# Attention, dense branch and residual added in PSUM: the sum in four column groups of TensorE instead of one

## The chip, the cores and the metric

The kernel runs on one core of a Trainium2 chip. The metric is the device time of one execution in microseconds. The kernel before took 192.61 us (median of 4 runs, 192.52 to 193.02). The engines are named as in the profile: PE is the matrix engine (PEld its weight loads, which have records of their own), DVE the vector engine, ACT the scalar engine, POOL the general one, and SP the engine that issues most DMA transfers here. PSUM is the accumulator memory that matmuls write, in banks; SBUF is the working memory.

## The reference

Two rows (one token of each of two batch entries, 448 numbers) are normalised, and two branches are added to the input:

```python
xn = _layernorm(x)                         # x: (2, 1, 448), bf16
# branch A: one query token against the last W = 4096 entries of a cache of 32768
q = (xn @ wq) -> 16 heads of 256;  k, v: 8 kv heads, each for two query heads
p = softmax(q k^T * 256**-0.5);  o = p v;  A = o.reshape(2, 4096) @ wo       # wo: (4096, 448)
# branch B: a dense layer with mish
h = xn @ w1 + b1;  B = (h * tanh(softplus(h))) @ w2                          # w1: (448, 1792)
out = x + A + B
```

Nearly all of the data is the window of the two caches: for each of 16 pairs of kv head and batch entry 4096 x 256 numbers of k and as many of v, 2 MB each. All inputs are bf16.

## The kernel before

**Loads.** All large loads go through the queue that SP issues. k has four buffers, v and the weights share five, wo has three. A pair's k and v tiles hold 32 cache entries on each of the 128 partitions. The order on SP is: wq (two parts), k of pair 0, w1, w2, k of pairs 1 and 2, and then in turn k two pairs ahead, v of this pair, and after each second pair that kv head's part of wo. The last v comes in three parts (half, a quarter, a quarter), the last wo in two (one for each of the kv head's two query heads), and these are the last loads.

**A pair.** Pairs are worked in two halves of 2048 cache entries. For each half DVE transposes k in 32x32 blocks (`turn`, L356), PE makes the scores with eight matmuls of 512 columns (`scores`, L368), ACT takes the exponential and row sums (L378), and DVE transposes the result (`turn_p`, L389). Two pairs later (`KA = 2`) `values` multiplies with v: 64 matmuls of two columns, whose weights are v itself (L415), into a tile `po`. DVE divides by the softmax's sum into `oT` (L426), which holds 128 partitions x 2 halves of the head x 2 query heads x 2 batch entries in bf16. When both batch entries of a kv head are done, `mix` multiplies `oT` by that kv head's part of wo.

**The sum.** All of the output's terms are added in PSUM, in two tiles `psA[0]` and `psA[1]` of 2 rows (batch entries) and 224 columns, in a bank each. The helper `add` (L206) is one matmul: the weights are two columns (one for each batch entry), and 224 columns of the other factor stream through. It is called for x itself (2 matmuls with an identity as weights), in `dense_out` for the dense branch (28, from pair 1 on in the order of work), and in `mix` (8 for each of 8 kv heads). In `mix` the loops run over query head, then bank, then half of the head, so that of the last eight matmuls the sixth ends bank 0 and the eighth bank 1.

**The end.** DVE copies `psA[0]` into columns 0 to 223 of `res`, ACT copies `psA[1]` into columns 224 to 447, and SP stores `res`, two rows of 896 bytes (L487 to L489).

**Order.** The instructions of each engine stand in the order of the program text; `issue_in_order` fixes it. An engine that waits holds up all that stands behind it.

Of the kernel before, what the change touches and what calls it, by code (L numbers as in the profile page):

```python
# [12 lines left out]
FP32 = mybir.dt.float32  # L13
# [21 lines left out]
def kernel(  # L35
# [13 lines left out]
    nc = tc.nc  # L49
    P = 128  # L50
    Q = 32
    NQ = P // Q

    Bsz, Sq, D = A_x.shape
    _, Hkv, Sk, Dh = A_k_cache.shape
    HqDh = A_wq.shape[1]
    Hq = HqDh // Dh
    rep = Hq // Hkv
# [12 lines left out]
    ND = Dh // P  # L71
# [8 lines left out]
    ident = lead.tile([P, P], BF16)  # L80
# [11 lines left out]
    ps_a = ctx.enter_context(tc.tile_pool(name="ps_a", bufs=1, space=PSUM))  # L92
# [3 lines left out]
    x_bf = consts.tile([Bsz, D], BF16)  # L96
# [5 lines left out]
    def v_tile(n):  # L102
        t = v_pool.tile([P, T * Dh], BF16, tag="v", name="v")
        return t[:, 0:n]
# [6 lines left out]
    for lo, hi in ((0, SC), (SC, NS)):  # L111
        w = v_tile((hi - lo) * HW).rearrange("p (s n) -> p s n", n=HW)
# [15 lines left out]
        out=rstd[:], in_=mv[:, 1:2], func=ACT.Sqrt, bias=eps_t[:], scale=1.0  # L128
# [5 lines left out]
    for r in range(2):  # L134
        n = (NS + 1 - r) // 2
        nc.vector.tensor_scalar(  # L136
            out=xn_bf[:, r : NS : 2, :, :],
# [12 lines left out]
    for b4 in range(NB):  # L150
        rows = slice(b4 * Q, (b4 + 1) * Q)
        for j in range(NQ):
            nc.vector.tensor_copy(
                out=spread[rows, b4, j * Q : (j + 1) * Q], in_=ident[rows, rows]
# [3 lines left out]
    for j in range(1, NQ):  # L158
        nc.vector.tensor_tensor(
            out=hsel, in0=hsel, in1=ident[:, j * Q : j * Q + rep], op=ALU.add  # L160
# [12 lines left out]
    for s in range(NS):  # L173
# [7 lines left out]
        out=odd[:],  # L181
        in_=ident[:].rearrange("p (u o) -> p o u", o=2),
# [4 lines left out]
    for par in range(2):  # L187
        for x in range(NX):
            which = (par + x) % 2
            nc.vector.tensor_scalar(  # L190
                out=xs[:, par : NS : 2, x, :],
# [6 lines left out]
    nc.vector.memset(ones[:], 1.0)  # L198


    NO = 2
    DO = D // NO
    psA = [ps_a.tile([Bsz, DO], FP32, name=f"psA{n}") for n in range(NO)]

    def add(n, lhsT, rhs, **flags):
        nc.tensor.matmul(psA[n][:, :], lhsT=lhsT, rhs=rhs, skip_group_check=True, **flags)  # L206

    for n in range(NO):
        add(n, ident[0:Bsz, 0:Bsz], x_bf[:, n * DO : (n + 1) * DO], start=True, stop=False)


    qrep = consts.tile([P, NB, HH, NE, NX, Bsz], BF16)
# [42 lines left out]
    act_bf = consts.tile([P, NF, NX, Bsz], BF16)  # L255
# [53 lines left out]
    def dense_out():  # L309
        w2_sb = dense.pop("w2")  # L310
        for x in range(NX):
            for c in range(NF):
                for n in range(NO):
                    add(
                        n,
                        act_bf[:, c, x, :],
                        w2_sb[:, x, c, n * DO : (n + 1) * DO],
                        start=False,
                        stop=False,
                    )  # L320


    NSTEP = len(heads) * NH
# [109 lines left out]
    def mix(kvh):  # L433
        oT = state["oT"]
        w = wo_t.pop(kvh)
        for h in range(rep):
            for n in range(NO):
                for c in range(ND):
                    add(
                        n,  # L440
                        oT[:, c, h, :],
                        w[:, h, c * D + n * DO : c * D + (n + 1) * DO],
                        start=False,
                        stop=(kvh == Hkv - 1 and h == rep - 1 and c == ND - 1),
                    )

    NK = len(heads)
    KA = 2
# [8 lines left out]
    for i in range(NK + KA):  # L457
        if i + 2 < NK:
            load_k(i + 2)
        if i < NK:  # L460
            load_v(i, (0, T) if i < NK - 1 else (0, T // 2, 3 * T // 4, T))
            kvh, b = heads[i]
            if b == Bsz - 1:
                load_wo(kvh, parts=1 if i < NK - 1 else 2)
            for half in range(NH):
                s = i * NH + half
                if s + 1 < NSTEP:
                    turn(s + 1)
                scores(s)
                if s >= 1:  # L470
                    turn_p(s - 1)
            if i + 2 < NK:
                build_q(i + 2)
        if i == NK:
            turn_p(NSTEP - 1)
        if i == 0:
            dense_in()
        if i == 1:
            dense_out()
        if i >= KA:  # L480
            values(i - KA)
            kvh, b = heads[i - KA]
            if b == Bsz - 1:
                mix(kvh)

    res = consts.tile([Bsz, D], BF16)
    nc.vector.tensor_copy(out=res[:, 0:DO], in_=psA[0][:, :])  # L487
    nc.scalar.copy(out=res[:, DO:D], in_=psA[1][:, :])  # L488
    nc.sync.dma_start(out=out.flatten_outer_dims(), in_=res[:])  # L489
    issue_in_order(tc)  # L490

# [29 lines left out]
```

The softmax here doesn't subtract the row's maximum and nothing guards it: scores larger than these inputs give would overflow.

## Time and profile before

| what | us |
| --- | --- |
| median of 4 runs | 192.61 (192.52 to 193.02) |
| the profiled execution, whole | 192.56 |
| its span from first to last instruction | 190.7 |
| PE busy, matmuls (1592) | 129.1 |
| DVE busy | 108.5 |
| ACT busy | 25.4 |
| last part of v has landed | 185.54 |
| last eight matmuls of the sum, start and length | 186.43, 1.67 |
| store issued | 188.49 |

The profile is one execution. A line of a timeline gives start and duration in microseconds, the engine, the line of the code, the operation, what it writes and reads with the shapes, and in brackets the idle time of the engine before it and what ended that. "128*2" at a matmul is rows x columns of the weights. "PEclk" and the clock column of windows are the clock that PE was granted: 1.00 is full, 0.50 half. Times that follow from single records are given to two or three decimals.

### The profile page before, as it was taken

Reading aid. Unit: us, or ns where it says so; the run is one execution under the profiler, and the core shown is the slowest. Engines: PE = TensorE matmul, PEld = TensorE weight load, DVE = VectorE, ACT = ScalarE, POOL = GpSimd, SP = SyncE. Lnnn points to the kernel's source line nnn. Section 1 sums busy time; section 2 is a strip of 40 time slices with the busy share of each in tenths; the row PEclk is TensorE's granted clock in tenths of the full one; section 3 lists DMA queues with packets and bytes.
Section 4 is the critical chain, followed back from the end, with each engine's and each line's share of the span. In section 5 each row is a group of like instructions: output and inputs, shape, how many; then the busy total and the mean of one; then the engine's idle time right before and its main releaser. Section 6 shows DMA issues by size and latency. Waiting matters only on the chain.

```text
span 190.7 us, 3752 instructions
## 1 busy us (share of the span) xinstructions
PE 129.1 (68%) x1592; PEld 75.7 (40%) x1592; DVE 108.5 (57%) x169; ACT 25.4 (13%) x69; POOL 25.1 (13%) x139
## 2 busy tenths in 40 slices
PE   0251991599876939397639766794949493895974
PEld 0151390145553616244334524361625333362672
DVE  4706406895949390939366663939092764849301
ACT  5000110111210211011100211021102011021100
POOL 8005220020220202002020202020200200000000
PEclk9999995769997996579856995599658879589965
DMA  6999999999999999999999999999999999999970
GB/s 231 424 436 418 432 435 426 426 428 421 431 438 423 430 416 440 426 426 417 449 426 419 423 433 431 430 440 419 426 423 430 421 442 423 437 425 431 402 280 7
DMA packets 7818, 77.90 MB, mean 409 GB/s; under 512 B 757, under 2 KB 2809, under 8 KB 3322
## 3 DMA queue, kind: packets, MB, share of 16 engines
q1 hardware_dynamic: 7796, 77.66, 96.3%
q8 instruction: 12, 0.20, 0.4%
q14 instruction: 4, 0.03, 0.0%
q10 hardware_dynamic: 6, 0.01, 0.0%
HBM read 77.67 MB, written 0.00 MB: 407 GB/s over the span
## 4 chain that ended last, share of the span: by engine, by line
DMA 81%; DVE 8%; PE 7%; SPq 1%; issue 0%; ACT 0%
DMA k<-in_A_k_cache_dram 67%; DMA v<-in_A_v_cache_dram 13%; DVE kt L356 6%; PE sc L368 3%; PE psA L206 3%; DVE pT L389 1%; PE o L415 1%; SPq L113 0%; SPq L260 0%; PE den L403 0%; SPq L265 0%; SPq L330 0%; DVE oT L426 0%; DVE den_sb L305 0%; ACT res L488 0%
## 5 line engine op out<-in xcount | busy, mean ns | idle before, releaser
L356 DVE STREAM_TRANSPOSE kt<-k 128x2048 f32<-128x2048 f32 x32 | 73.5, 2299 | 44.0 <-DMA k<-in_A_k_cache_dram 44.0
L368 PE MATMUL sc<-kt,qdiag 128*128 128x512 bf16 x256 | 76.5, 451 | 15.5 <-DVE kt L356 15.5
L368 PEld LDWEIGHTS <-qdiag 128*128 128x128 bf16 x256 | 26.8, 113 | 51.9 <-issue 32.3
L378 ACT ACTIVATE p<-sc 128x512 bf16<-128x512 f32 x32 | 19.1, 598 | 143.6 <-PE sc L368 139.1
L249 POOL COPY qdiag<-qrep 32x8 bf16<-32x8 bf16 x128 | 21.1, 187 | 123.2 <-PE sc L368 108.6
L415 PEld LDWEIGHTS <-v 128*128 128x128 bf16 x1024 | 29.0, 99 | 5.9 <-issue 2.2
L415 PE MATMUL o<-pT,v 128*128 128x2 bf16 x1024 | 28.9, 164 | 1.0 <-DMA v<-in_A_v_cache_dram 1.0
L206 PE MATMUL psA<-wo,oT 128*2 128x224 bf16 x64 | 11.9, 357 | 18.6 <-DVE oT L426 18.6
L389 DVE STREAM_TRANSPOSE pT<-p 128x512 bf16<-128x512 bf16 x32 | 21.5, 671 | 0.0
L206 PEld LDWEIGHTS <-oT 128*2 128x2 bf16 x64 | 6.2, 107 | 21.6 <-DVE oT L426 19.3
L403 PE MATMUL den<-sums,ones_f 128*128 128x2 f32 x32 | 5.5, 242 | 13.0 <-DVE sums L399 13.0
L403 PEld LDWEIGHTS den<-sums,ones_f 128*128 128x128 f32 x32 | 5.6, 198 | 19.1 <-DVE sums L399 17.7
L405 DVE RECIPROCAL rec<-den 128x2 f32<-128x2 f32 x16 | 2.7, 171 | 16.5 <-PE den L403 16.5
L220 PE MATMUL qT_ps<-xs,v 128*128 128x4 bf16 x112 | 3.3, 166 | 5.3 <-DMA v<-in_A_wq_dram 2.8
L426 DVE TENSOR_TENSOR oT<-o,rec 128x4 bf16<-128x4 f32 x16 | 2.2, 135 | 7.4 <-PE o L415 7.4
L378 ACT ACTIVATION_READ_ACCUMULATOR p<-sc 128x1 f32 x32 | 6.2, 194 | 0.0
L220 PEld LDWEIGHTS <-v 128*128 128x128 bf16 x112 | 3.1, 104 | 5.8 <-DMA v<-in_A_wq_dram 5.8
L174 PE MATMUL xnT_ps<-ident,xn_bf 2*128 2x2 bf16 x7 | 0.5, 166 | 5.2 <-DVE xn_bf L136 5.2
L399 DVE SCALAR_TENSOR_TENSOR sums<-hsel,rs,sums 128x2 f32<-128x2 f32 x16 | 3.5, 221 | 0.6
L229 DVE CAST qT<-qT_ps 128x64 bf16<-128x64 f32 x1 | 0.2, 224 | 6.2 <-PE qT_ps L220 6.2
L275 PE MATMUL hT_ps<-xs,v 128*128 128x4 bf16 x49 | 3.7, 195 | 0.0
L206 PE MATMUL psA<-v,act_bf 128*2 128x224 bf16 x28 | 3.5, 290 | 0.0
(43 smaller groups left out, 29.4 us busy)
## 6 DMA issues: line engine op xcount, KB each, us to landing
k<-in_A_k_cache_dram SPq DMA_DIRECT2D x16, 2048.0 KB, 32.1
v<-in_A_v_cache_dram SPq DMA_DIRECT2D x15, 2048.0 KB, 35.1
v<-in_B_w_dram SPq DMA_DIRECT2D x2, 1568.0 KB, 21.1
wo<-in_A_wo_dram SPq DMA_DIRECT2D x7, 448.0 KB, 32.1
v<-in_A_wq_dram SPq DMA_DIRECT2D x1, 2048.0 KB
v<-in_A_wq_dram SPq DMA_DIRECT2D x1, 1536.0 KB, 10.5
v<-in_A_v_cache_dram SPq DMA_DIRECT2D x1, 1024.0 KB, 29.0
v<-in_A_v_cache_dram SPq DMA_DIRECT2D x2, 512.0 KB, 27.4
```

What stands on the lines that cost most here:

```text
L206: nc.tensor.matmul(psA[n][:, :], lhsT=lhsT, rhs=rhs, skip_group_check=True, **flags)
L220: nc.tensor.matmul(qT_ps[:, hh, e, :], lhsT=wq_v[s][:, hh, e, :], rhs=xs[:, s, :, :].rearrange("p x b -> p (x b)"), start=(s == 0), stop=( ...
L249: nc.gpsimd.tensor_copy(out=tv[rows, :, e, j * Q : j * Q + rep], in_=qrep[rows, :, h0 : h0 + rep, e, x, b],)
L275: nc.tensor.matmul(hT_ps[:, c, :, :].rearrange("p x b -> p (x b)"), lhsT=w1_v[:, s, c, :], rhs=xs[:, s, :, :].rearrange("p x b -> p (x b)" ...
L356: nc.vector.transpose(out=kt[:].bitcast(FP32), in_=k[:, half * TH * Dh : (half + 1) * TH * Dh].bitcast(FP32),)
L368: nc.tensor.matmul(psc[:], lhsT=qdiag[i % NW][:, n * NE + e, :], rhs=ktv[:, n, e, :, :], start=(n == 0 and e == 0), stop=(n == NB - 1 and ...
L378: nc.scalar.activation(out=p_sb[:], in_=psc[:].rearrange("p t c -> p (t c)"), func=ACT.Exp, scale=scale, accum_out=state["rs", i][:, s % N ...
L389: nc.vector.transpose(out=pT[:], in_=p_t.pop(s)[:])
L399: nc.vector.scalar_tensor_tensor(out=sums[:], in0=hsel, scalar=rs[:, 1:2], in1=sums[:], op0=ALU.mult, op1=ALU.add)
L403: nc.tensor.matmul(den[:], lhsT=ones_f[:], rhs=sums[:], start=True, stop=True)
L405: nc.vector.reciprocal(out=state["rec", i][:], in_=den[:])
L415: nc.tensor.matmul(po[:, c, :], lhsT=vv[:, t, c, :], rhs=pTv[:, th, 0:rep], start=(t == 0 and c == 0), stop=(t == T - 1), skip_group_check ...
```

## The change

The two PSUM tiles now have 128 partitions and 112 columns. Each holds two column groups: group n is rows 32 n and 32 n + 1, in tile n // 2. `add` makes four matmuls of 112 columns where it was called twice for 224, and names for each the column group of the array (`tile_position=(0, n * Q)`, Q = 32). All four have the same weights, which are loaded for each of them, into the columns of that group. In `mix` the loops are query head, half of the head, column group. At the end there are four copies, two by DVE out of the first tile and two by ACT out of the second, each from two rows of a group into the two rows of `res`; the store is as before.

PE has 188 weight loads and matmuls of the sum instead of 94; DVE and ACT have one copy more each. Nothing changes on SP and POOL. Each of the last four matmuls ends a column group, in the order 0, 1, 2, 3, and each copy waits for its own group.

```diff
-    NO = 2
+    NO = NQ
     DO = D // NO
-    psA = [ps_a.tile([Bsz, DO], FP32, name=f"psA{n}") for n in range(NO)]
-
-    def add(n, lhsT, rhs, **flags):
-        nc.tensor.matmul(psA[n][:, :], lhsT=lhsT, rhs=rhs, skip_group_check=True, **flags)
-
-    for n in range(NO):
-        add(n, ident[0:Bsz, 0:Bsz], x_bf[:, n * DO : (n + 1) * DO], start=True, stop=False)
+    psA = [ps_a.tile([P, DO], FP32, name=f"psA{u}") for u in range(2)]
+
+    def part(n):
+        return psA[n // 2][n * Q : n * Q + Bsz, :]
+
+    def add(lhsT, w, start=False, stop=False):
+        for n in range(NO):
+            nc.tensor.matmul(
+                part(n),
+                lhsT=lhsT,
+                rhs=w[:, n * DO : (n + 1) * DO],
+                start=start,
+                stop=stop,
+                tile_position=(0, n * Q),
+                skip_group_check=True,
+            )
+
+    add(ident[0:Bsz, 0:Bsz], x_bf[:, :], start=True)
...
-                for n in range(NO):
-                    add(
-                        n,
-                        act_bf[:, c, x, :],
-                        w2_sb[:, x, c, n * DO : (n + 1) * DO],
-                        start=False,
-                        stop=False,
-                    )
+                add(act_bf[:, c, x, :], w2_sb[:, x, c, :])
...
-            for n in range(NO):
-                for c in range(ND):
-                    add(
-                        n,
-                        oT[:, c, h, :],
-                        w[:, h, c * D + n * DO : c * D + (n + 1) * DO],
-                        start=False,
-                        stop=(kvh == Hkv - 1 and h == rep - 1 and c == ND - 1),
-                    )
+            for c in range(ND):
+                add(
+                    oT[:, c, h, :],
+                    w[:, h, c * D : (c + 1) * D],
+                    stop=(kvh == Hkv - 1 and h == rep - 1 and c == ND - 1),
+                )
...
-    nc.vector.tensor_copy(out=res[:, 0:DO], in_=psA[0][:, :])
-    nc.scalar.copy(out=res[:, DO:D], in_=psA[1][:, :])
+    for n in range(NO):
+        copy = nc.vector.tensor_copy if n // 2 == 0 else nc.scalar.copy
+        copy(out=res[:, n * DO : (n + 1) * DO], in_=part(n))
     nc.sync.dma_start(out=out.flatten_outer_dims(), in_=res[:])
```

## The prediction

> **What bounds the kernel now.** I read the slices of the span first, to see which resource is full, then the chain of work that ended last, to see what stands behind the last transfer, and then the end of the span instruction by instruction. The slices:
>
> ```profile
> span 190.7 us, 3752 instructions
> PE   0251991599876939397639766794949493895974
> DVE  4706406895949390939366663939092764849301
> DMA  6999999999999999999999999999999999999970
> GB/s 231 424 436 418 432 435 426 426 428 421 431 438 423 430 416 440 426 426 417 449 426 419 423 433 431 430 440 419 426 423 430 421 442 423 437 425 431 402 280 7
> ```
>
> The transfers are at 90% or more of their engines from the second slice to the 38th, at 402 to 449 GB/s; PE and DVE are not. So 77.9 MB have to come in, and what PE does beside that stream costs nothing as long as it doesn't delay a load. The changed matmuls occur beside it many times and behind it once. The chain, for the end of the span (start, duration, what):
>
> ```profile
> 159.95 25.59 DMA v<-in_A_v_cache_dram
> 185.54 0.05 issue
> 185.59 0.60 PE o L415 x16
> 186.19 0.02 issue
> 186.22 0.18 DVE oT L426
> 186.39 0.04 issue
> 186.43 1.67 PE psA L206 x8
> 188.10 0.02 issue
> 188.12 0.34 ACT res L488
> ```
>
> Only what follows 185.54 can be shortened by this change: sixteen value matmuls, the division, eight matmuls into the sum, one copy. The same stretch as a timeline (start, duration, engine, line, what, idle before):
>
> ```profile
> 186.43 1.21 PEld L206 LDWEIGHTS <-oT 128*2 128x2 bf16 x8 [0.34 <-DVE oT L426]
> 186.43 1.65 PE L206 MATMUL psA<-wo,oT 128*2 128x224 bf16 x8 [0.26 <-DVE oT L426]
> 187.75 0.38 DVE L487 CAST res<-psA 2x224 bf16<-2x224 f32 x1 [1.37 <-PE psA L206]
> 188.12 0.34 ACT L488 CAST res<-psA 2x224 bf16<-2x224 f32 x1 [9.24 <-PE psA L206]
> 188.49 0.32 SPq L489 DMA_DIRECT2D out_dram<-res  x1
> ```
>
> Bank 0 is complete one matmul ahead of bank 1, so DVE's copy lies beside the last matmul; ACT's copy is on the path. From the store's issue at 188.49 to the end of the span are 2.2 us of store and final synchronisation, which stay. The granted clock in this stretch, by windows (last three figures: clock, DMA share, GB/s):
>
> ```profile
> 186.00:187.00 1.00, 0.74 (x11) 0.48 (x9) 0.17 (x1) 0.00 (x0) 0.00 (x0) 0.50 0.05 18
> 187.00:188.00 1.00, 1.00 (x6) 0.46 (x4) 0.25 (x1) 0.00 (x0) 0.00 (x0) 0.50 0.00 0
> ```
>
> PE runs at half clock here. The starts of these eight matmuls lie 187 ns apart (0.83 ns per column of 224), and the last takes 391 ns. In the same burst at 179.99 us, at clock 1.00, they lie 95 ns apart. Their spacing is the streaming of columns, and halves with the clock.
>
> **The change, part by part.** The sum's 94 matmuls of 224 columns become 188 of 112, each with its weight load. DVE and ACT get one copy more each; the loads, the store and their order on SP, and POOL, are as before.
>
> *Beside the stream: taken at nothing.* The first add (2 matmuls at 5.62, later 4) is covered by PE's wait for wq; the dense product (28, 41.02 to 44.47) and seven bursts of eight are covered by DMA at a share of 0.93 to 1.10 in every 2 us from 30 to 70 us. In one place cover is thin: behind the dense product the chain reaches the k load at 52.22, for whose issue SP waited 1.3 us on the transposes. Other loads filled the engines meanwhile (1.02 and 1.05 in the windows before and after), so neither an earlier nor a later issue by 1 or 2 us shows; I allow 0.2 us either way for a changed order of transfers. If PE were the limit there, the dense product's 3.4 us would count in full.
>
> *The last sum, 16 matmuls for 8.* The trace shows no matmuls on other column groups of the array, so the period between starts must be bounded. From below: the value matmuls (L415) change weights each time as well and use all 128 rows; in the sixteen at 185.59, at the same half clock, starts lie 26.6 ns apart while each lasts 165. From above, if groups take turns: 112 x 0.83 = 93 ns. Further up, if a weight load waits for the matmul in front of it: 79 ns (shortest load of this line) + 93 = 172. I take 26.6: streaming holds only the columns that it uses, successive matmuls use four different groups, and one group comes round every 4 x 26.6 = 106 ns, longer than its 93. One matmul lasts 165 + 93 = 258.
>
> Then a new wait comes in. The eight matmuls of the second head need the second half of wo, whose last completion is in the trace at 186.66; the matmul that needs it started at 187.14 in before and would be ready at 186.43 + 0.05 + 7 x 0.027 = 186.67 now. With the 0.04 from completion to PE that the last v load shows (185.54 to 185.59) it starts at 186.70. The last matmul, seven later, starts at 186.89 and ends at 187.15, against 188.09: **-0.94 us**. All of PE that follows stands behind that wait, and both copies with it.
>
> *Copies.* ACT: 335 ns for 2x224. With the slope between its 128x28 (226) and 128x512 (598) rows, 0.77 ns a column, 112 columns take 249, and two of them 0.50. The first waits for group 2, 0.03 before the last matmul. DVE: 379 for 224 columns; by its 128x64 and 128x256 casts out of PSUM (224 and 424, 1.04 ns a column) 262 each. Whether the second overlaps the first is open: the sixteen 32x32 copies of L153 start 77 ns apart within a block of rows and 171 ns apart, the whole of a copy, where the block changes. I take no overlap, 0.54, since the copies here change their block of PSUM rows. DVE goes from 187.10 to 187.65, ACT from 187.16 to 187.67, and the store is issued at 187.70 instead of 188.49. Beside the 0.94 won, 0.15 goes to the copies: **-0.79 us** in all. With the overlap of L153 on both engines it would be -0.86.
>
> The profiled execution took 192.56 with its span of 190.7; it stands 0.05 under the median of the four runs (192.61). 192.56 - 0.79 = 191.77, or 191.82 by the median: I say 191.8.
>
> **Where the Trainium skill speaks against it.** The trace shows loads of this line beside its matmuls (1.21 us of loads inside the 1.65), all on the same rows. "TensorE: Matmul & The Clock Gate", section "Part 3: Packing small matmuls — row/col tiling", says that a weight load overlaps matmuls in flight only where the row group differs; here it never does. By that rule the sum would be the 172 ns of the third bound, and the kernel slower; the trace of before contradicts it for one column group, and the same section reports 2.38x for three column tiles. On the copies the rows of L153 come first, and "VectorE: DVE Perf Modes", section "Two Vector instructions with no wait between them", adds that an instruction whose input starts in another 32-partition quadrant than the last one's is held until that has finished. By it DVE's two take 0.54 and not 0.46; ACT ends later anyway, so the sum is the same by either.
>
> **The rivals.**
> - *Groups take turns* (period 93). For it: no row shows two groups at once. Against it: the column streams are independent in everything that L415 shows. Sixteen periods of 93 are eight of 187, so PE ends as before; the first ACT copy starts one period ahead of the last matmul, so the copies cost 0.50 - 0.09 - 0.335 = +0.07. Time: 192.7, the change doesn't do what it says.
> - *Weight loads serialise* (the other side). One mechanism, in the last burst: load, then matmul, at 172 ns, or 219 with this line's long loads of 126. For it: the loads of L206 lengthen from 79 to 126 when matmuls are in flight. Against it: they still end before the next matmul starts. Price: 14 x (172 - 93) = +1.1 us to 14 x (219 - 93) = +1.8, so 193.7 to 194.4. It decides from a period of about 120 ns, where the end is 0.4 us later.
> - *Clock at 1.00 in the last burst.* The forecast changes little, since the period is not the streaming any more: the last matmul takes 165 + 48 instead of 258, 191.75. With turns as well, the period is 47 ns and the time about 192.1. For it: the burst at 179.99. Against it: the clock fell at 182, before anything that the change touches in that stage.
>
> **How the numbers follow.** A measurement of this kernel tells about 0.2%, 0.39 us, from no change. Chances: forecast 0.66, including periods of up to 60 ns (14 x 33 ns = +0.47 at most, so 191.4 to 192.2 with the transfers' 0.2); turns 0.15; serialised loads 0.12; the last transfers landing otherwise by over 0.4 us, 0.07, both signs. Faster 0.67, same 0.17, slower 0.16. The range reaches from the forecast's lower end, with the copies overlapped, to the case of turns plus 0.2: 191.3 to 192.9. The forecast's own range is 191.4 to 192.2.
>
> **What would show it.** In the last burst: sixteen L206 matmuls of 112 columns in 0.7 us instead of 1.65, with a wait for wo before the ninth; starts about 27 ns apart, 93 for turns, 170 and more for serialised loads. Two copies each on DVE and ACT, 0.5 us in all, after the last matmul. The store's issue 2.1 us behind the last v landing rather than 2.9. I am wrong if the starts lie over 60 ns apart, or if v's last landing moves by more than what the tail gains.

## The result

The changed kernel takes 191.99 us (median of 43 runs, 191.72 to 193.14) against 192.65 us before (64 runs, 192.35 to 193.28). The ratio is 0.9974, 95% interval 0.9966 to 0.9981: faster by 0.26%. The forecast was 191.8, so the sign, the range (191.3 to 192.9) and the forecast's own range (191.4 to 192.2) hold, and 0.66 us came of the 0.79 that the sum had.

The median hides what the single times show. They fall into two groups with nearly nothing between them: 33 of 43 lie at 191.72 to 192.37, with a median of 191.87, and 10 at 192.70 to 193.14, with a median of 192.97. Before has no second group: none of 136 executions, over all comparisons, is above 193.28. The lower group is 0.78 us under before, the forecast's gain almost to the digit; the upper one is slower than before. So there are two questions: is the gain what the forecast says it is, and what is the upper group?

### The profile page after: what moved, and what is told of

Its sections match the earlier page's. It is cut to its first block, busy times and chain, and to the rows that moved or that the text cites. A ratio compares the mean times of both kernels' runs of the same rounds, so it can differ in the third digit from the quotient of the medians.

```text
span 191.1 us, 3942 instructions
## 1 busy us (share of the span) xinstructions
PE 126.9 (66%) x1686; PEld 72.7 (38%) x1686; DVE 108.6 (57%) x170; ACT 25.6 (13%) x70; POOL 25.1 (13%) x139
## 4 chain that ended last, share of the span: by engine, by line
DMA 70%; DVE 15%; PE 11%; SPq 1%; issue 1%; ACT 0%; ACTq 0%
DMA k<-in_A_k_cache_dram 70%; DVE kt L361 11%; PE sc L373 6%; PE o L420 4%; DVE pT L394 3%; PE psA L211 1%; PE den L408 1%; DVE sums L404 1%; SPq L113 0%; DVE oT L431 0%; DVE sums L401 0%; SPq L277 0%; SPq L272 0%; SPq L335 0%; DVE den_sb L317 0%
## 5 line engine op out<-in xcount | busy, mean ns | idle before, releaser
L373 PE MATMUL sc<-kt,qdiag 128*128 128x512 bf16 x256 | 84.4, 487 | 14.0 <-DVE kt L361 14.0
L373 PEld LDWEIGHTS <-qdiag 128*128 128x128 bf16 x256 | 28.8, 121 | 53.7 <-issue 36.5
L420 PEld LDWEIGHTS <-v 128*128 128x128 bf16 x1024 | 28.3, 98 | 4.7 <-issue 1.8
L420 PE MATMUL o<-pT,v 128*128 128x2 bf16 x1024 | 28.2, 163 | 0.6 <-issue 0.6
L211 PE MATMUL psA<-wo,oT 128*2 128x112 bf16 x128 | 4.2, 277 | 23.8 <-DVE oT L431 23.8
L408 PEld LDWEIGHTS den<-sums,ones_f 128*128 128x128 f32 x32 | 7.1, 246 | 19.2 <-DVE sums L404 18.5
L408 PE MATMUL den<-sums,ones_f 128*128 128x2 f32 x32 | 6.4, 269 | 11.3 <-DVE sums L404 11.3
L211 PEld LDWEIGHTS <-oT 128*2 128x2 bf16 x128 | 2.2, 100 | 24.5 <-DVE oT L431 24.5
L232 PEld LDWEIGHTS <-v 128*128 128x128 bf16 x112 | 3.2, 104 | 6.3 <-DMA v<-in_A_wq_dram 6.3
L287 PEld LDWEIGHTS <-v 128*128 128x128 bf16 x49 | 3.2, 151 | 0.3
```

The costliest lines, as they stand in the source:

```text
L211: nc.tensor.matmul(part(n), lhsT=lhsT, rhs=w[:, n * DO : (n + 1) * DO], start=start, stop=stop, tile_position=(0, n * Q), skip_group_check ...
L232: nc.tensor.matmul(qT_ps[:, hh, e, :], lhsT=wq_v[s][:, hh, e, :], rhs=xs[:, s, :, :].rearrange("p x b -> p (x b)"), start=(s == 0), stop=( ...
L287: nc.tensor.matmul(hT_ps[:, c, :, :].rearrange("p x b -> p (x b)"), lhsT=w1_v[:, s, c, :], rhs=xs[:, s, :, :].rearrange("p x b -> p (x b)" ...
L373: nc.tensor.matmul(psc[:], lhsT=qdiag[i % NW][:, n * NE + e, :], rhs=ktv[:, n, e, :, :], start=(n == 0 and e == 0), stop=(n == NB - 1 and ...
L408: nc.tensor.matmul(den[:], lhsT=ones_f[:], rhs=sums[:], start=True, stop=True)
L420: nc.tensor.matmul(po[:, c, :], lhsT=vv[:, t, c, :], rhs=pTv[:, th, 0:rep], start=(t == 0 and c == 0), stop=(t == T - 1), skip_group_check ...
```

## The profile after

The profiled execution is one of the upper group: 192.86 us, span 191.1. First its chain of work that ended last, from 182.6 us on (start, duration, what):

```profile
182.90 0.38 PE den L408 x2
183.28 2.20 PE o L420 x84
185.48 0.62 issue
186.10 1.32 PE o L420 x44
187.42 0.02 issue
187.45 0.17 DVE oT L431
187.62 0.04 issue
187.66 0.65 PE psA L211 x12
188.32 0.23 ACT res L491
188.55 0.27 ACTq L519
```

Before, this stretch hung on v's last landing. Here no DMA is in it: from 182.90 on PE waits for no load, so PE has become the late one. And in the middle of the value matmuls, after 84 of 128, PE stands still for 0.62 us with "issue" as the reason: it waited for nothing that the profile shows. The last burst of the sum and what follows, as a timeline:

```profile
187.66 0.28 PEld L211 LDWEIGHTS <-oT 128*2 128x2 bf16 x16 [0.34 <-DVE oT L431]
187.66 0.54 PE L211 MATMUL psA<-wo,oT 128*2 128x112 bf16 x16 [0.26 <-DVE oT L431]
188.24 0.56 DVE L491 CAST res<-psA 2x112 bf16<-2x112 f32 x2 [0.62 <-PE psA L211]
188.31 0.52 ACT L491 CAST res<-psA 2x112 bf16<-2x112 f32 x2 [7.53 <-PE psA L211]
188.88 0.34 SPq L492 DMA_DIRECT2D out_dram<-res  x1
```

The changed part does what it should: sixteen matmuls in 0.54 us where eight took 1.65, the copies in 0.56, and the store issued 1.21 us after the first matmul instead of 2.05. PE's lateness is older than that. The windows of after and then of before show the clock in the last score matmuls (third figure from the right):

```profile
176.00:178.00 2.00, 1.97 (x6) 0.99 (x7) 0.78 (x2) 0.00 (x0) 0.00 (x0) 0.50 1.00 426
178.00:180.00 2.00, 2.00 (x10) 0.73 (x8) 0.00 (x0) 0.00 (x0) 0.00 (x0) 0.50 0.95 403
```

```profile
176.00:178.00 2.00, 1.99 (x11) 1.01 (x11) 0.78 (x2) 0.00 (x0) 0.00 (x0) 1.00 0.97 410
178.00:180.00 2.00, 1.74 (x66) 1.66 (x65) 0.23 (x2) 0.69 (x2) 0.00 (x0) 1.00 0.97 410
```

At 0.50 instead of 1.00 the eight score matmuls of the last half take 3.57 us instead of 1.90 (again after, then before):

```profile
176.48 3.57 PE L373 MATMUL sc<-kt,qdiag 128*128 128x512 bf16 x8
```

```profile
176.26 1.90 PE L368 MATMUL sc<-kt,qdiag 128*128 128x512 bf16 x8
```

The last thing to see is a DMA queue that the profile calls "instruction" (first before, then after, part 3 of each page):

```profile
q8 instruction: 12, 0.20, 0.4%
```

```profile
q8 instruction: 13, 0.21, 0.4%
```

Each of these packets holds 16 KB. The change adds 188 instructions to PE, and with them a thirteenth packet, so this document takes the packets to be parts of PE's program; no trace shows that directly. The stop is no wait for the thirteenth packet, which starts after it, at 187.22. The packet ahead of the stop is the twelfth, from 183.78 to 184.70, and the kernel before has that one too.

## Experiments

A run of the changed kernel that falls in the lower group is needed to read the rest; it comes first.

**The changed kernel again.** Nothing edited.

> The changed kernel once more, on this chip. Two groups of times, about three quarters at 191.7 to 192.4 and one quarter at 192.7 to 193.1; the stop of PE at the same place (the twenty-first value matmul of the last pair) in either, hidden by the wait for v in the lower group.

Twelve executions: eight at 191.81 to 192.34, four at 192.72 to 193.25, about as expected. The profiled one is of the lower group (192.15 us, span 190.4). Its timeline from the value matmuls of the last two pairs on:

```profile
181.78 2.44 PE L420 MATMUL o<-pT,v 128*128 128x2 bf16 x84
184.85 0.88 PE L420 MATMUL o<-pT,v 128*128 128x2 bf16 x28 [0.62 <-issue]
185.97 0.59 PE L420 MATMUL o<-pT,v 128*128 128x2 bf16 x16 [0.24 <-DMA v<-in_A_v_cache_dram]
186.81 0.68 PE L211 MATMUL psA<-wo,oT 128*2 128x112 bf16 x16 [0.26 <-DVE oT L431]
188.16 0.33 SPq L492 DMA_DIRECT2D out_dram<-res  x1
```

The same stop, after the same 84th matmul, 0.62 us long. But here PE came to it at 184.2 and not at 185.5; after it PE still waits 0.24 for v's last part. The stop is covered. The last half's scores took 1.90 us here. The store is issued 0.72 us earlier than in the upper execution, and the two executions differ by 0.71.

**Is the gain the concurrency of the groups?** The same 188 matmuls, all in column group 0:

```diff
-    psA = [ps_a.tile([P, DO], FP32, name=f"psA{u}") for u in range(2)]
+    psA = [ps_a.tile([Bsz, 2 * DO], FP32, name=f"psA{u}") for u in range(2)]
-        return psA[n // 2][n * Q : n * Q + Bsz, :]
+        return psA[n // 2][:, (n % 2) * DO : (n % 2 + 1) * DO]
-                tile_position=(0, n * Q),
...
+    nc.vector.tensor_copy(out=res[:, 0 : 2 * DO], in_=psA[0][:, :])
+    nc.scalar.copy(out=res[:, 2 * DO : D], in_=psA[1][:, :])
```

> The sum in 188 matmuls of 112 columns as in the changed kernel, but all in column group 0, so that nothing can run side by side; two copies of 224 columns at the end as before. If the gain is the concurrency of the groups: starts 93 ns apart, last burst 1.65 us, 192.65 us as before (within 0.2). If the gain comes from anything else in the change (smaller matmuls, another order of the loops, other clocks), it stays: 191.9.

192.81 us (12 runs), ratio to before 1.0021 (1.0006 to 1.0036). The burst is back at its old length:

```profile
186.71 1.65 PE L211 MATMUL psA<-wo,oT 128*2 128x112 bf16 x16 [0.26 <-DVE oT L430]
```

So the gain is the concurrency and nothing else in the change. Its profile has the stop too (0.50 us, covered). Four of the twelve are at 193.55 to 193.98: the upper group is there without any concurrency, 0.9 us over the rest.

**Two groups of 224 columns.** As many matmuls as before, one copy on each engine:

```diff
-    NO = NQ
+    NO = 2
-        return psA[n // 2][n * Q : n * Q + Bsz, :]
+        return psA[n][n * Q : n * Q + Bsz, :]
-        copy = nc.vector.tensor_copy if n // 2 == 0 else nc.scalar.copy
+        copy = nc.vector.tensor_copy if n == 0 else nc.scalar.copy
```

> Two column groups of 224 columns, one in each bank, 94 matmuls as before, one copy of 224 columns on DVE and one on ACT. If groups run side by side: eight matmuls in four rounds of 187 ns, the last burst about 0.95 us, the store's issue 1.35 us after the first of them (2.05 before, 1.21 in the changed kernel), 191.95 us. If only four groups do so, or the spacing is set otherwise: 192.65. If the executions of the changed kernel at 193.0 come from its longer program, there are few or none here; if they come from the shorter sum, as many as there (10 of 43).

191.99 us (9 runs, 191.75 to 192.43), ratio 0.9964 (0.9952 to 0.9977).

```profile
186.79 0.91 PE L211 MATMUL psA<-wo,oT 128*2 128x224 bf16 x8 [0.26 <-DVE oT L431]
187.73 0.38 DVE L491 CAST res<-psA 2x224 bf16<-2x224 f32 x1 [1.00 <-PE psA L211]
188.19 0.34 SPq L492 DMA_DIRECT2D out_dram<-res  x1
```

Eight matmuls in four rounds, 0.91 us; the store 1.40 after the first. There is no stop in PE's program and no upper group. Run again for more executions:

> The kernel of e2_two_groups again, for more executions: its program is as long as that of the kernel before, so none at 192.7 or above; median 191.9 to 192.0, no more than 0.15 over e10_more_code_again.

191.85 us (5 runs, 191.77 to 192.07; 191.9 to 192.0 was expected), ratio 0.9961 (0.9949 to 0.9973). None of 14 executions in all is above 192.43. Half the concurrency brings nearly all of the gain.

**Is the stop a matter of the program's length?** Two kernels have more PE instructions at 5.5 us, where PE waits anyway. The changed kernel with 63 more transposes, so that the same work stands 126 instructions later in the program:

```diff
-    for s in range(NS):
+    for s in [j % NS for j in range(10 * NS)]:
         nc.tensor.transpose(
             xnT_ps[:, s, :],
```

> The changed kernel with the seven transposes of xn done ten times over (63 more transposes at 5.5 us, where PE waits for wq), so that the place in the program where PE stood still for 0.62 us in the last value matmuls lies 126 instructions earlier in the work. If that stop is a fetch of the program: no stop in the last value matmuls, and the upper executions are at most 0.6 us above the others (192.5), median 191.85. If it belongs to the work at that place (v, the clock, the pair's data): the stop stays, and a quarter of the executions stay at 193.0.

192.05 us (5 runs, 191.82 to 192.17), ratio 0.9965 (0.9953 to 0.9977), somewhat over the expected 191.85. There is no stop in the last value matmuls; they wait for v alone:

```profile
181.21 1.84 PE L420 MATMUL o<-pT,v 128*128 128x2 bf16 x64
183.22 1.01 PE L420 MATMUL o<-pT,v 128*128 128x2 bf16 x32 [0.16 <-DMA v<-in_A_v_cache_dram]
```

And the kernel before with 91 more (`14 * NS` in the same place), 3319 instructions against the changed kernel's 3325:

> The kernel before with 91 more transposes of xn at 5.5 us, which makes its PE program as long as that of the changed kernel (3319 and 3325 instructions) with the same end. If the length of the program makes the upper executions: some at about 0.6 us over the highest of before (193.8), median 192.65 to 192.75. If the shorter sum makes them: the same times as before, 192.65, none above 193.3.

192.92 us (12 runs, 192.42 to 193.48), ratio 1.0016 (1.0003 to 1.0029). Five of twelve are at 193.35 to 193.48, where no execution of the plain kernel before lies. They are 0.7 to 0.8 us above the median of the other seven (192.69), and 0.2 above the highest of before, not the 0.6 that was expected; the median, too, is over the expected 192.65 to 192.75. Its profile, of a covered execution, has the stop now (79 matmuls, and its "issue"):

```profile
181.18 2.51 PE L415 MATMUL o<-pT,v 128*128 128x2 bf16 x79
183.98 1.02 PE L415 MATMUL o<-pT,v 128*128 128x2 bf16 x33 [0.28 <-issue]
```

So the stop goes with the place in the program, not with the work: it comes with length, in a kernel without column groups. The single records agree. In all six profiles that have the stop (the changed kernel twice, one group, before with more code, and two below) PE stops behind the same record of its trace, the 3265th of loads and matmuls in order of start, and in each a 16 KB packet had started 2.2 to 2.5 us and ended 1.28 to 1.54 us before PE went on. The kernel before has 3200 such records and never comes so far. In the four profiles with the longer front (this one and three below) PE passes the 3265th record without a stop; the packet ahead of it had started 5.8 to 9.6 us earlier. So the place alone doesn't make the stop: it is there where PE comes to that place soon after the packet. That PE waits for this packet fits all ten profiles, but it is read from the times alone.

The upper group goes with the kernels that have the stop. With it, and with the scores as they were, 23 of 79 executions are upper ones (14 of 55 of the changed kernel over both series, 4 of 12 with one group, 5 of 12 of before with more code). Without it there is no second group in before (136), two groups (14) and the longer front (10, with the repeat below). One group, two groups and both longer programs ran on one chip, so it is no matter of the chip.

**Does the upper group need a late PE as well?** Half of the last pair's score matmuls left out, and as many transposes put in at the start, so that the tail lies at the same place in the program:

```diff
-    for s in range(NS):
+    for s in [j % NS for j in range(NS + 2 * NB)]:
...
-        for n in range(NB):
+        nb = NB if i < len(heads) - 1 else NB // 2
+        for n in range(nb):
...
-                    stop=(n == NB - 1 and e == NE - 1),
+                    stop=(n == nb - 1 and e == NE - 1),
```

> The changed kernel without half of the last pair's score matmuls (four of eight in each half, so these scores are incomplete), and with as many transposes more at 5.5 us, so that the PE program is as long as before and its tail lies at the same instructions. PE reaches the last value matmuls 1 to 3 us earlier. If the upper executions need both a late PE and the stop in its program: none at 193.0, all between 191.7 and 192.4. If the stop alone makes them: a quarter at 193.0 still.

191.98 us (5 runs, 191.82 to 192.11), ratio 0.9962 (0.9950 to 0.9974). The last scores ran at half clock in this profile and the stop of 0.36 us is there, yet PE is ahead of v. Five executions are few against a group that holds a quarter; the next pair is the stronger test.

**A PE that is always late, with and without the stop.** The last half's eight score matmuls done twice:

```diff
-        for n in range(NB):
+        again = 2 if s == NSTEP - 1 else 1
+        for n in [j % NB for j in range(again * NB)]:
```

> The changed kernel with the eight score matmuls of the very last half done twice (the second pass starts the accumulation anew, so the scores are the same), which makes PE late by 1.9 us at full clock, as late as in the execution at 192.9 us. If that execution is slow because a late PE meets the stop in its program: nearly all executions at 192.9 to 193.3 now, more where the doubled matmuls run at half clock (3.6 us). If lateness alone is not enough: the lower group stays at 191.8 to 192.4.

193.12 us (12 runs), ratio 1.0044 (1.0023 to 1.0065): eight at 192.74 to 193.26, four at 194.23 to 194.66. None is left in the lower group. The same with the longer front:

> The same doubled matmuls together with the longer front of e3_after_more_code, so that the late PE meets no stop in the last value matmuls. If the 1.1 us of the upper group are 0.6 of lateness and 0.6 of the stop: most at 192.3 to 192.6, 0.5 to 0.7 under e8_late_pe. If lateness alone is the price: as e8_late_pe.

192.22 us (12 runs), ratio 1.0008 (0.9981 to 1.0035): eight at 191.92 to 192.25, four at 193.66 to 194.21. The expectation failed here (most at 192.3 to 192.6, 0.5 to 0.7 under the kernel with the stop), and tells something: the lateness of one doubled half alone costs less than 0.1 us, not 0.5 to 0.7 (the lower eight have a median of 192.08; the longer front without doubling, 192.05 in ten executions). The upper four of each are probably too late for any cover; none of them was profiled. The two chains, first with the stop and then without:

```profile
182.84 0.59 PE den L409 x2
183.42 2.03 PE o L421 x76
185.45 0.33 issue
185.78 1.54 PE o L421 x52
```

```profile
182.72 0.38 PE den L409 x2
183.11 3.28 PE o L421 x128
```

The stop has moved from the 84th matmul to the 76th, by just the eight pairs of instructions that were put in ahead of it: once more it is the place in the program. Of the 0.93 us between the two ends (187.32 and 186.39) the stop is 0.33. Another 0.21 is the denominator's matmuls and 0.29 the value matmuls, at a lower clock (0.50 from 182.7 on, where the other had 1.00 until 185); the rest is a later start. Why the clock was lower in this one the runs don't tell. So a late PE with the stop costs 0.9 us more than a late PE without it (median 193.02 of the lower eight against 192.08), and only a third of that is shown to be the stop itself.

**The longer front again,** for more executions:

> The kernel of e3_after_more_code again, for more executions: none at 192.7 or above if the upper group needs the stop, a quarter if it does not; median 191.85 to 192.05.

192.05 us (5 runs, 191.75 to 192.15), ratio 0.9967 (0.9955 to 0.9980). With the first run, none of 10 is above 192.17, against 14 of 55 at 192.70 or above for the changed kernel.

**One copy on each engine.** On the kernel with the longer front (192.05): copies of 34 rows that take in two groups each, PSUM set to zero at the start for the rows between, and the output stored from the groups' rows by two queues:

```diff
-    res = consts.tile([Bsz, D], BF16)
...
+    res = consts.tile([P, DO], BF16)
+    nc.vector.tensor_copy(out=res[0 : Q + Bsz, :], in_=psA[0][0 : Q + Bsz, :])
+    nc.scalar.copy(out=res[2 * Q : 3 * Q + Bsz, :], in_=psA[1][2 * Q : 3 * Q + Bsz, :])
+    for b, queue in ((0, nc.sync), (1, nc.scalar)):
+        queue.dma_start(
+            out=out.flatten_outer_dims()[b : b + 1, :].rearrange("o (n c) -> (o n) c", n=NO),
+            in_=res[b : 3 * Q + b + 1 : Q, :],
+        )
```

> The changed kernel with the longer front of e3_after_more_code, one copy on DVE (rows 0 to 33 of the first bank, with PSUM set to zero at the start) and one on ACT (rows 64 to 97 of the second), side by side, and the output stored from the four groups' rows, a row of the output by SP's queue and one by ACT's, in four pieces of 224 bytes each. If the second copy on each engine is on the path: the stores' issue comes 0.26 to 0.3 us earlier after the first matmul of the last burst (0.9 instead of 1.2 us), 191.55 us. If the pieces of 224 bytes or a second store cost as much as the copies did, 191.85 or more.

193.11 us (11 runs), ratio 1.0016 (1.0008 to 1.0025): slower than before, and about 1 us over the kernel that it was made from.

```profile
187.21 0.27 DVE L491 CAST res<-psA 34x112 bf16<-34x112 f32 x1 [0.71 <-PE psA L213]
187.55 0.62 ACTq L494 DMA_DIRECT2D out_dram<-res  x1
187.55 0.65 SPq L494 DMA_DIRECT2D out_dram<-res  x1
```

The copies did get shorter, and the stores are issued 1.0 us after the first matmul of the burst at 186.55 (1.35 in the lower execution of the changed kernel). But from there to the end of the span are 3.4 us (187.55 to 190.93) instead of 2.2 (188.16 to 190.37): the stores take twice as long to issue, and the end of the span comes later behind them. Which of the two, the pieces of 224 bytes or the second queue, costs more was not taken apart.

## Why the prediction was right, and where it was not

**The last burst: right in kind, too careful in size.** The forecast took 27 ns between starts as the bound that the value matmuls gave. The four groups' matmuls start within 10 ns of each other, and from the second round on a round follows every 93 ns, the streaming of 112 columns in one group. Unhindered the sixteen take 0.54 us; the forecast had 0.68 without the wait. Both rivals with a longer period fall. The forecast's own range of 191.4 to 192.2 isn't quite what its terms give: with 0.07 less for overlapped copies, 0.47 more for the longer period and 0.2 either way it is 191.5 to 192.5. The measured median lies in either.

The Trainium skill's rule that was weighed there ("TensorE: Matmul & The Clock Gate", section "Part 3: Packing small matmuls — row/col tiling": loads overlap matmuls in flight only where the row group differs) disagrees with this measurement: four loads for the same 128 rows start 3.4 ns apart and their matmuls run at the same time. The measurement decides.

**The new wait for wo: right.** The trace of the lower execution has the last completion of wo at 187.09 and the ninth matmul at 187.13. Without that wait it would have started at about 186.96, an estimate from the upper execution, where wo has long landed and the ninth starts 0.14 us after the first. The burst is 0.68 instead of 0.54 for it. What the forecast lost by the larger period, it had back in this wait (0.17 us here, 0.03 in the forecast), and that is luck: -0.94 was forecast for PE's end, and 0.97 came (1.65 to 0.68).

**The copies: right to 0.05 in length, later in time.** DVE's two take 261 and 266 ns and ACT's 245 and 247, 292 and 269 apart from start to start, so neither overlaps: 0.56 and 0.52 (forecast 0.54 and 0.50). For DVE that agrees with what the prediction took from the skill's page on VectorE. But the groups end together, so the copies start behind the whole burst: from PE's end to the store's issue are 0.67 us where the forecast had 0.55. From the burst's first matmul to the store the gain is 0.7 us (2.05 to 1.35), not 0.79. That the lower group's median comes to 0.78 is in part luck: v's last part landed at 185.54 in the profile before and at 185.92 here, more than the 0.2 that the forecast allowed for transfers.

**"Beside the stream: taken at nothing": this is the step that failed.** It asked whether 94 more pairs have the time, and PE has it. It did not ask where their code comes from. With 188 instructions more, the last value matmuls lie across the 3265th record of PE's trace, a place that the kernel before, with 3200, doesn't reach. In the lower execution the stop there is covered by the wait for v; where PE comes late, it stands on the path. That the upper group comes with the place of the last value matmuls in the program is shown, by before with more code (five of twelve) and by the changed kernel moved along its program (none of ten). That the stop alone isn't enough is shown by the profiles in which it is covered; that a late PE with it is enough, and mostly not without it, by the pair with doubled scores (none of twelve in the lower group with the stop, eight of twelve without it). What makes PE late in a quarter of the executions is seen in one profile only, the scores at half clock. PE's mean granted clock over an execution, which is on record for each, speaks for it: it is 0.828 in 9 of the 14 upper executions and in none of the 41 others, and 0.826 to 0.828 in the five upper ones of before with more code and in none of the other seven. But the profiled upper execution (0.793) isn't one of these; that PE is late by its clock in all of them is likely and not shown. In the sum: ten of the 43 executions cost 1.1 us more than the others; the median moves by 0.12, from 191.87 to 191.99, and the mean by 0.24, from 191.94 to 192.18.

**The clock.** The rival with full clock in the last burst did not occur: it was 0.50 in both profiles of the changed kernel. In the upper one the clock mattered 10 us earlier, where the forecast did not look.

## What to carry to other kernels

Matmuls whose weights have only two columns ran side by side here when they were put in several column groups, and the burst behind the last load shrank from 1.65 us to 0.54, or 0.68 with the wait for wo. Take no more groups than the next limit needs: with two groups, and no instruction more than before, the kernel is as fast (191.96 median of 14) and steadier than with four, since the next waits (the last part of wo, the copies) take what the others win. And count what an edit adds to an engine's program, not only to its time: read single execution times as well as the median, for an edit that adds some two hundred instructions made a stop here that only some executions paid.

## What the runs showed that was not expected

- PE stopped for 0.28 to 0.62 us at a fixed place in its program, in every profile of a kernel with 1683 to 1694 matmuls in its trace, each with a load, and in none of the kernels with 1592 or with 1749 and more. It went on 1.28 to 1.54 us after a 16 KB packet of the "instruction" queue had ended. The stop lies in a stretch where a load and a matmul follow every 25 to 27 ns; no stop came where the packet had started 5.8 us or more before PE got there.
- Matmuls in four column groups, all with 128 rows, started within 10 ns of each other; the value matmuls, which use the whole array one after another, start 25 to 27 ns apart.
- A store of two pieces of 896 bytes by one queue ended the span 2.2 us after its issue; two stores of four pieces of 224 bytes each, on two queues, 3.4 us.
